# A two-level Winograd kernel: the first partial sum of seven gate stages copied into PSUM by ScalarE, their products reordered and the inner sums spread

## The chip, the cores and the metric

The kernel runs on one core of one Trainium2 chip. A core has TensorE (PE in the profile; its weight loads are PEld), VectorE (DVE), ScalarE (ACT), GpSimd (POOL) and SyncE (SP, which issues most transfers). Each engine runs its own instructions in order and waits for others on semaphores. TensorE writes its products to PSUM, eight banks of 512 fp32 values in each of 128 partitions; VectorE and ScalarE read them there.

The metric is the device time of one execution in microseconds (us), as the median of several runs.

## The reference

All inputs are fp32. For 8 batches of 8 heads, 576 tokens and a head dimension of 64:

```python
kv  = einsum('bhsd,bhse->bhde', k, v)
out = einsum('bhsd,bhde->bhse', q, kv)
x   = out / sqrt(mean(out * out, axis=-1) + 1e-6) * g_norm   # then as (4608, 512)
a, b = x @ w1, x @ w2                                        # (4608, 1024) each
result = (a * b @ w3) @ w_out                                # (4608, 512)
```

## The kernel before, in words

**Stages.** The kernel first multiplies `w3` and `w_out` into one matrix `w3o` of 1024 x 512. The 4608 tokens are then worked in nine groups T of 512 tokens. Groups 0 to 7 hold the first 512 tokens of each batch, group 8 the 64 left over from every batch; the order is 0 to 6, then 8, then 7. For each group there are the two gates (`x @ w1`, `x @ w2`, multiplied elementwise into `ab`) and a projection (`ab` times `w3o`). The attention of batch T + 1 runs in pieces between the products of group T, by the callback `between`.

**One-level gates.** `gates(T, p, ...)` makes two of the eight blocks of 128 gate columns, p and p + 4, with `winograd` (lines 698 to 746): the 2 x 2 blocks c11, c12, c21, c22 from seven products in place of eight. Each product is four matmuls of 128x128 weights by 256 tokens (eight rows in the profile) and fills one bank: one half for `w1`, one for `w2`. A product may be added to what another left in its bank. `keep` (L726) is a copy of a bank to SBUF by ScalarE. `done` calls `multiply`: for a sum of two partial sums VectorE adds them (L859) and multiplies the two halves (L860); where the whole sum is in one bank, ScalarE copies one half (L854) and VectorE multiplies it with the other (L856). The seven products use three banks, r1, r2 and r3, out of a pool of five that hands them out in turn.

**The seven groups with two levels.** In the groups T = 2 to 6, 8 and 7 (`IN_TWO`) p = 2 is made first with one level, then p = 0 and 1 with two levels (`gates_of_two`), and at last p = 3 with one level. Only this last stage is touched. Before the change its order on PE is

```python
a11 b11 -> r1, copied by ScalarE (p1);  s1 t1 -> r2, copied (p5);  s2 t2 added to r1, copied (u2)
# between(): in T = 2 to 5 the next batch's k v products (L335) and their six copies (L343, L345)
s4 b22 added to r2, c12 done;  s3 t3 added to r1, c22 done (adds p5 and r1);  a12 b21 -> r3, c11 done (adds r3 and p1)
a22 t4 added to r1, c21 done
```

**The sums behind.** The projection of these groups (`project_twice`, matmuls at L1223) has two levels too: seven outer products n = 0 to 6, each with seven inner ones of blocks of 128. For that VectorE forms the outer sums of p = 3 (`sum_ab`, L766 and L767), the last of the outer sums of p = 0 to 2 (`of_two`, L1072; the others are L1069 to L1071), and the inner sums of each outer operand (`sum_inner`, L1181 to L1185: three sums s1, s2, s4, and one block replaced by a difference). `sum_inner(0)` belongs to c11, `sum_inner(1, 2)` to the outer sums s1 and s2 in double width. The dictionary `following` (line 1487) says which of them run after which of the four blocks is done.

**What sets the order.** PE, POOL and SP run in the order in which the code is written. In these stages VectorE does too (`manual_schedule`). ScalarE's instructions are placed by the scheduler; the copies that belong to the attention (L294, L296 and L308 for q and x, L343 and L345 for k v) are hung behind certain copies of the gates (`run_slot`).

Of the kernel before, what the change touches and what calls it, by code (L numbers as in the profile page):

```python
# [22 lines left out]
def kernel(  # L23
# [32 lines left out]
    nc = tc.nc  # L56
# [27 lines left out]
    def bank(pool, tag):  # L84
        return pool.tile([P, 512], FP32, name=tag, tag=tag)
# [433 lines left out]
    def run_slot(key, behind):  # L519
        for f, *args in slots.pop(key, []):  # L520
            with tc.issue_after(behind.ins):
                f(*args)
# [174 lines left out]

    def winograd(
        lhsT, rhs, chunks, done, between=lambda: None, keep_u3=True, after=lambda: None,
        places=(2, 1, 0),  # L700
    ):


        def product(a_name, b_name, to=None):
            ps = to if to is not None else bank(ps_mm, "mm").rearrange("p (u n) -> p u n", u=2)
            for u in range(2):
                for c in range(chunks):
                    nc.tensor.matmul(  # L708
                        ps[:, u, :],
                        lhsT=lhsT(a_name, u, c),  # L710
                        rhs=rhs(b_name, c),

                        start=(u == 0 and c == 0 and to is None),
                        stop=(c == chunks - 1),
                        skip_group_check=True,
                    )
            after()
            return ps

        def keep(name, ps):  # L720
            if name == "p1":
                t = pair_of_sums[:, 0].rearrange("p s c t -> p (s c) t")
            else:
                t = late_slots(places[("p5", "u2", "u3").index(name)])
            t = t[:, 0:4, :].rearrange("p (u a) n -> p u (a n)", u=2)
            copies.setdefault(name, []).append(nc.scalar.copy(t, ps))  # L726
            run_slot((stage[0], name), copies[name][-1])
            late[name] = t
            return t

        r1 = product("a11", "b11")
        p1 = keep("p1", r1)
        r2 = product("s1", "t1")
        p5 = keep("p5", r2)
        product("s2", "t2", r1)
        u2 = keep("u2", r1)
        between()
        product("s4", "b22", r2)
        done("c12", r2, u2)
        product("s3", "t3", r1)  # L740
        done("c22", p5, keep("u3", r1) if keep_u3 else r1)
        r3 = product("a12", "b21")
        done("c11", r3, p1)
        between()
        product("a22", "t4", r1)
        done("c21", r1, None)
# [84 lines left out]
    def sum_ab(p):  # L831
        aa[p] = {f"a{i + 1}{j + 1}": ab[j][:, p, i, :] for i in range(2) for j in range(2)}
        return sums(aa[p], free["ab", p])
# [10 lines left out]
    def gates(T, p, between, ready=lambda name: None):  # L844
        def done(name, one, two):
            multiply(name, one, two)
            ready(name)

        def multiply(name, one, two):

            dst = ab[int(name[1]) - 1][:, p, int(name[2]) - 1, :]
            if two is None:
                c = late_pool.tile([P, N], FP32, name="c21")
                copied = nc.scalar.copy(c, one[:, 0, :])  # L854
                run_slot((stage[0], name), copied)
                adds.setdefault(name, []).append(nc.vector.tensor_mul(dst, c, one[:, 1, :]))  # L856
                return
            c = late_pool.tile([P, 2, N], FP32, name="c")
            adds.setdefault(name, []).append(nc.vector.tensor_add(c, one, two))  # L859
            nc.vector.tensor_mul(dst, c[:, 0, :], c[:, 1, :])  # L860

        winograd(
            lambda name, w, c: wa[p][name][:, w, c, :],
            lambda name, c: xb[T][name][:, c, :],
            NP // 2, done, between, T == 0 or p + 1 < NF,
            places=(2, 1, 0) if T not in IN_TWO else (0, 1, 2) if p + 1 == NF else (2, 0, 1),
        )


# [287 lines left out]

    inner = {}

    def sum_inner(*ns, between=lambda: None):  # L1160

        x_1 = ab[1].rearrange("p f j n -> p j f n")
        if ns == (1, 2):
            x = two_ab_sums[0]
        elif ns == (5, 6):
            x = x_1
        else:
            n, = ns
            x = {0: ab[0][:, :, 0], 3: ab_sums[2], 4: ab[0][:, :, 1], 6: x_1[:, 1]}[n].unsqueeze(1)
        a11, a12, a21, a22 = (  # L1170
            x[:, :, 2 * j:2 * j + 2, i * P:(i + 1) * P] for i in range(2) for j in range(2)
        )
        if len(ns) == 2:
            s1, s2, s4 = (pair_of_sums[:, :, i] for i in range(3))
        else:
            s1, s2, s4 = (
                t.unsqueeze(1) for t in (
                    inner_sums[n % 4 // 3] if n < 6 else [pair_of_sums[:, 0, i] for i in range(3)]
                )
            )  # L1180
        nc.vector.tensor_add(s1, a21, a22)  # L1181
        nc.vector.tensor_sub(s2, s1, a11)
        nc.vector.tensor_sub(s4, a12, s2)
        between()
        nc.vector.tensor_sub(a21, a11, a21)  # L1185
        for i, n in enumerate(ns):
            inner[n] = [t[:, i] for t in (a11, a12, a22, s1, s2, s4, a21)]

    def project_twice(T, last, ahead, load_after):
        def store(half):  # L1190
# [245 lines left out]
    for n, T in enumerate(groups):  # L1436
# [44 lines left out]
        for p in range(NF):  # L1481
            if T in IN_TWO and p + 1 < NF:
                continue
            stage[0] = f"p{p}" if T in IN_TWO or T == FIRST_OF_TWO - 1 else None
            if T and p + 1 == NF:
                sum_1, sum_2, sum_4, sum_3 = sum_ab(p)
                following = {
                    "c12": [], "c22": [sum_1], "c11": [lambda: sum_inner(0, between=sum_2)],
                    "c21": [*of_two, lambda: sum_inner(1, 2), sum_3, sum_4],
                }  # L1490
                if T not in TWICE:
                    in_order = tc.manual_schedule(engines={mybir.EngineType.DVE})
                    in_order.__enter__()
                gates(T, p, between, lambda name: all_of(f() for f in following[name]))
                continue
            gates(T, p, between if T or p else lambda: None)
            if T == 0:

                def begin_early(behind):
                    t = early.pop(0)  # L1500
                    with tc.issue_after(behind.ins):
                        next(t)
                    next(t)

                if p == 0:
                    begin_early(copies["xT"])
                if p + 1 < NF:
                    ops = sum_w(p + 1)
                    if p != 2:
                        ops.pop(0)()  # L1510
                    with tc.issue_after(adds["c12"][p].ins):
                        run(ops)
                for n in range(2):
                    if len(converted) < len(todo):
                        ahead = [copies["p5"][p] if p else copies["xT"], copies["u3" if p == 1 else "u2"][p]][n]
                        with tc.issue_after(ahead.ins):
                            begin_next()
                        if len(begun) < len(todo):
                            with tc.issue_after(adds["c12"][0].ins):
                                if p:  # L1520
                                    for c in begun[len(converted)]:
                                        next(c)
                                else:
                                    end_next()
                if p == 0:
                    begin_early(copies["u3"][0])
                if p + 1 == NF:
                    allocate_projection()
                    first, *others = zip(*(f(i) for i in range(NF) for f in (sum_ab, combine_w3o)))
                    with tc.issue_after(adds["c21"][p - 2].ins):  # L1530
                        all_of(step() for step in first)
                    with tc.issue_after(adds["c12"][p - 1].ins):
                        all_of(step() for steps in others for step in steps)
            else:
                ops = [step() for step in sum_ab(p)]
                with tc.issue_after(ops[-1].ins):
                    if p == 1:
                        prepare_some(3)
# [52 lines left out]
```

## Time and profile before

| | |
|---|---|
| runs | 746.61 us median of 3 (745.99 to 747.71) |
| the profiled execution | 747.45 us, of which the span from first to last instruction is 745.7 us |
| granted TensorE clock | 1.000 |
| PE busy | 737.3 us (99%), 6843 matmul rows |
| VectorE busy | 632.7 us (85%), 1212 instructions |
| ScalarE busy | 371.2 us (50%), 638 instructions |
| mean DMA rate | 228 GB/s |

The windows view around the stage that is touched, in T = 3: its first three products, the k v products, its last four products, and the projection. The columns after the window are its length and the busy time of PE, PEld, VectorE, ScalarE and POOL with the number of instructions, then the granted clock, the DMA share and GB/s:

```profile
350.98:356.16 5.18, 5.18 (x26) 4.38 (x24) 5.15 (x12) 3.07 (x6) 0.00 (x0) 1.00 0.92 338
356.16:357.46 1.30, 1.30 (x73) 1.14 (x73) 1.30 (x3) 1.30 (x3) 0.00 (x0) 1.00 0.69 277
357.46:364.47 7.01, 7.01 (x38) 6.19 (x33) 5.92 (x11) 2.81 (x8) 0.00 (x0) 1.00 0.85 153
364.47:386.35 21.88, 21.88 (x197) 21.88 (x196) 20.70 (x42) 8.40 (x12) 0.00 (x0) 1.00 0.91 313
```

PE is busy in all of each window. A busy share is an average, and matmuls are pipelined with modelled ends: a matmul that starts late can still look busy, so the length of a stage of equal matmuls is a second thing to compare. In the views of waits a line reads: who waited, for whom, us in total, times, longest. In the views in order of time it reads: start, duration, engine, source line, operation, what it writes from what, form, and in brackets the idle time before it with what ended it.

### The profile page before, as it was taken

Reading aid. Unit: us, or ns where it says so; the run is one execution under the profiler, and the core shown is the slowest. Engines: PE = TensorE matmul, PEld = TensorE weight load, DVE = VectorE, ACT = ScalarE, POOL = GpSimd, SP = SyncE. Lnnn points to the kernel's source line nnn. Section 1 sums busy time; section 2 is a strip of 40 time slices with the busy share of each in tenths; the row PEclk is TensorE's granted clock in tenths of the full one; section 3 lists DMA queues with packets and bytes.
Section 4 is the critical chain, followed back from the end, with each engine's and each line's share of the span. In section 5 each row is a group of like instructions: output and inputs, shape, how many; then the busy total and the mean of one; then the engine's idle time right before and its main releaser. Section 6 shows DMA issues by size and latency. Waiting matters only on the chain.

```text
span 745.7 us, 16769 instructions
## 1 busy us (share of the span) xinstructions
PE 737.3 (99%) x6843; PEld 658.5 (88%) x6843; DVE 632.7 (85%) x1212; ACT 371.2 (50%) x638; POOL 21.5 (3%) x29
## 2 busy tenths in 40 slices
PE   8999999999999999999999999999999999999998
PEld 5455788888899999999999999999999999999997
DVE  6987998967868699979996999799969987997797
ACT  6687878414552575256526752575267313212321
POOL 0000000131000000010000000000001000000000
PEclk9999999999999999999999999999999999999999
DMA  9996934598999689968987898579847672465454
GB/s 310 365 308 215 263 107 122 124 333 288 275 310 329 172 218 268 312 165 233 276 284 169 252 295 270 179 240 265 290 107 218 209 224 87 157 228 166 133 199 136
DMA packets 135456, 169.65 MB, mean 228 GB/s; under 512 B 78036, under 2 KB 110804, under 8 KB 135380
## 3 DMA queue, kind: packets, MB, share of 16 engines
q1 hardware_dynamic: 132928, 154.16, 68.9%
q10 hardware_dynamic: 2452, 14.42, 5.6%
q8 instruction: 54, 0.88, 0.5%
q14 instruction: 22, 0.18, 0.1%
HBM read 130.55 MB, written 20.71 MB: 203 GB/s over the span
## 4 chain that ended last, share of the span: by engine, by line
PE 94%; DMA 2%; DVE 1%; ACT 1%; issue 0%; SPq 0%; ACTq 0%; DVEq 0%
PE mm L708 38%; PE mm L1223 22%; PE mm L976 21%; PE mm L682 7%; PE at L335 2%; PE at L413 1%; DMA raw<-in_moe_w_out_dram 1%; PE at L669 1%; DMA w3o_sb<-w3o_l 1%; PE mm L413 1%; DMA raw<-in_moe_w_dram 0%; PE at L1266 0%; PE at L432 0%; ACT w_sb L133 0%; DVE c L859 0%; ACT qT L296 0%
## 5 line engine op out<-in xcount | busy, mean ns | idle before, releaser
L1025 ACT COPY slots<-mm 128x512 f32<-128x512 f32 x88 | 51.6, 586 | 131.4 <-PE mm L1223 73.4
L708 PE MATMUL mm<-xT,w_sb 128*128 128x256 f32 x480 | 110.2, 379 | 0.0
L708 PEld LDWEIGHTS mm<-xT,w_sb 128*128 128x128 f32 x480 | 90.4, 190 | 12.1 <-issue 0.5
L708 PE MATMUL mm<-xc,ws 128*128 128x256 f32 x352 | 79.8, 380 | 0.9 <-ACT inner_sums L726 0.9
L708 PEld LDWEIGHTS mm<-xc,ws 128*128 128x128 f32 x352 | 66.9, 190 | 10.2 <-ACT inner_sums L726 1.3
L726 ACT COPY slots<-mm 128x512 f32<-128x512 f32 x61 | 35.8, 587 | 70.9 <-PE mm L708 66.7
L682 PE MATMUL mm<-chunks,ab 128*128 128x512 f32 x128 | 60.7, 605 | 1.2 <-DVE chunks L172 1.2
L1029 DVE TENSOR_TENSOR slots<-mm,slots 128x512 f32<-128x512 f32 x66 | 45.3, 686 | 17.7 <-PE mm L976 17.3
L1026 ACT COPY slots<-mm 128x384 f32<-128x384 f32 x88 | 42.4, 482 | 24.9 <-PE mm L1223 22.3
L976 PE MATMUL mm<-ws,w3o_sb 128*128 128x128 f32 x350 | 54.0, 275 | 0.0
L1223 PE MATMUL mm<-w3o_sb,ab 128*128 128x128 f32 x368 | 48.7, 275 | 0.2 <-DMA w3o_sb<-w3o_l 0.2
L976 PEld LDWEIGHTS mm<-ws,w3o_sb 128*128 128x128 f32 x350 | 46.4, 192 | 0.0
L1223 PEld LDWEIGHTS mm<-w3o_sb,ab 128*128 128x128 f32 x368 | 45.4, 192 | 0.8 <-issue 0.4
L381 DVE TENSOR_REDUCE inv<-sq 128x8 f32<-128x512 f32 (+1 forms) x40 | 24.5, 628 | 25.3 <-ACT sq L380 25.0
L1223 PE MATMUL mm<-w3o_sb,raw 128*128 128x128 f32 x340 | 43.5, 275 | 0.0
L708 PE MATMUL mm<-xc,w_sb 128*128 128x256 f32 x176 | 42.4, 384 | 0.3 <-ACT slots L726 0.3
L682 PEld LDWEIGHTS mm<-chunks,ab 128*128 128x128 f32 x128 | 21.6, 190 | 22.9 <-issue 14.3
L1223 PEld LDWEIGHTS mm<-w3o_sb,raw 128*128 128x128 f32 x340 | 40.7, 192 | 0.0
L708 PE MATMUL mm<-xT,ws 128*128 128x256 f32 x160 | 38.5, 384 | 0.0
L708 PEld LDWEIGHTS mm<-xc,w_sb 128*128 128x128 f32 x176 | 32.8, 190 | 5.3 <-ACT slots L726 0.7
L1030 DVE TENSOR_TENSOR slots<-mm,slots 128x384 f32<-128x384 f32 x66 | 36.4, 551 | 0.9 <-PE mm L1223 0.9
L854 ACT COPY c<-mm 128x256 f32<-128x256 f32 x22 | 8.2, 371 | 54.1 <-PE mm L708 51.2
(230 smaller groups left out, 1634.2 us busy)
## 6 DMA issues: line engine op xcount, KB each, us to landing
w3o_sb<-w_l SPq DMA_DIRECT2D x21, 896.0 KB, 5.3
w3o_sb<-w3o_l SPq DMA_DIRECT2D x18, 896.0 KB, 4.7
raw<-in_moe_w_dram SPq DMA_DIRECT2D x31, 512.0 KB, 7.8
raw<-w3o_l SPq DMA_DIRECT2D x15, 896.0 KB, 4.8
w3o_sb<-w3o_l ACTq DMA_DIRECT2D x14, 896.0 KB, 4.7
k_sb<-in_k_dram SPq DMA_DIRECT2D x16, 576.0 KB, 4.9
v_sb<-in_v_dram SPq DMA_DIRECT2D x16, 576.0 KB, 6.1
q_sb<-in_q_dram SPq DMA_DIRECT2D x32, 256.0 KB, 4.5
```

The lines of the kernel that those rows point to most:

```text
L335: nc.tensor.matmul(ps[r * D:(r + 1) * D, :], lhsT=k_sb[rows, r, cols], rhs=v_sb[rows, r, cols], start=(j == 0), stop=(j == JS - 1),)
L381: adds["norm"] = nc.vector.tensor_reduce(out=inv[:, i], in_=sq.rearrange("p (h d) -> p h d", d=D), axis=AX.X, op=ALU.add)
L413: nc.tensor.matmul(o_ps[l][tokens, n * D:(n + 1) * D], lhsT=qT[r][rows, e, i, tokens], rhs=kv_b[rows, m // 2 ^ l, e, h, :], start=True, st ...
L682: nc.tensor.matmul(sums_ps[half][m], lhsT=w3T[half, c][:, m, :], rhs=chunks[:, c, 1, :], start=(c == 0), stop=(c == KF - 1),)
L708: nc.tensor.matmul(ps[:, u, :], lhsT=lhsT(a_name, u, c), rhs=rhs(b_name, c),  start=(u == 0 and c == 0 and to is None), stop=(c == chunks ...
L726: copies.setdefault(name, []).append(nc.scalar.copy(t, ps))
L976: nc.tensor.matmul(ps[place // 4][:, place % 4, :], lhsT=x, rhs=y, start=new and place // 4 not in seen, stop=True, skip_group_check=True,)
L1025: nc.scalar.copy(z[:, 0:4], ps[0])
L1026: return nc.scalar.copy(z[:, 4:7], ps[1][:, 0:3])
L1029: nc.vector.tensor_add(z[:, 0:4], ps[0], z[:, 0:4])
L1030: nc.vector.tensor_add(z[:, 4:7], ps[1][:, 0:3], z[:, 4:7])
L1223: nc.tensor.matmul(ps[place // 4][:, place % 4, :], lhsT=x[:, c, :], rhs=y[:, c, :], start=new and place // 4 not in seen, stop=(c == 1), ...
```

## The change

In the last one-level gates of the seven groups (`copy_first`), the products run in another order. `a11 b11` goes to r1, ScalarE copies it into r3, another PSUM bank, and `a12 b21` is then added there by PE, so that c11 lies whole in one bank and is made as c21 is: a copy of one half by ScalarE and a multiplication by VectorE. The order of the blocks becomes c11, c22, c12, c21 (before: c12, c22, c11, c21). `sum_inner` is split into steps, and the inner sums of the outer operands 0, 1 and 2 are made one by one (before: 0 alone, 1 and 2 together) and set between the other work after each block, as the new `following` lists. The copy of P1 in SBUF is gone. Line numbers of the changed kernel that matter: L712 matmuls of `winograd`, L739 the copy into r3, L880 and L882 a block from one bank, L885 and L886 a block from two, L1216 to L1219 the steps of an inner sum, L1262 the projection's matmuls.

```diff
--- before.py
+++ after.py
@@ -697,12 +697,16 @@
 
     def winograd(
         lhsT, rhs, chunks, done, between=lambda: None, keep_u3=True, after=lambda: None,
-        places=(2, 1, 0),
+        places=(2, 1, 0), copy_first=False, first=None,
     ):
 
 
-        def product(a_name, b_name, to=None):
-            ps = to if to is not None else bank(ps_mm, "mm").rearrange("p (u n) -> p u n", u=2)
+        def halves(ps):
+            return ps.rearrange("p (u n) -> p u n", u=2)
+
+        def product(a_name, b_name, to=None, new=False):
+            new = new or to is None
+            ps = halves(bank(ps_mm, "mm")) if to is None else to
             for u in range(2):
                 for c in range(chunks):
                     nc.tensor.matmul(
@@ -710,7 +714,7 @@
                         lhsT=lhsT(a_name, u, c),
                         rhs=rhs(b_name, c),
 
-                        start=(u == 0 and c == 0 and to is None),
+                        start=(u == 0 and c == 0 and new),
                         stop=(c == chunks - 1),
                         skip_group_check=True,
                     )
@@ -727,6 +731,28 @@
             run_slot((stage[0], name), copies[name][-1])
             late[name] = t
             return t
+
+        if copy_first:
+            r1 = halves(first if first is not None else bank(ps_mm, "mm"))
+            r3 = halves(bank(ps_mm, "mm"))
+            product("a11", "b11", r1, new=True)
+            copies["p1"].append(nc.scalar.copy(r3, r1))
+            run_slot((stage[0], "p1"), copies["p1"][-1])
+            r2 = product("s1", "t1")
+            p5 = keep("p5", r2)
+            product("s2", "t2", r1)
+            u2 = keep("u2", r1)
+            between()
+            product("a12", "b21", r3)
+            done("c11", r3, None)
+            product("s3", "t3", r1)
+            done("c22", p5, r1)
+            product("s4", "b22", r2)
+            between()
+            done("c12", r2, u2)
+            product("a22", "t4", r1)
+            done("c21", r1, None)
+            return
 
         r1 = product("a11", "b11")
         p1 = keep("p1", r1)
@@ -864,6 +890,8 @@
             lambda name, c: xb[T][name][:, c, :],
             NP // 2, done, between, T == 0 or p + 1 < NF,
             places=(2, 1, 0) if T not in IN_TWO else (0, 1, 2) if p + 1 == NF else (2, 0, 1),
+            copy_first=T in IN_TWO and p + 1 == NF,
+            first=None,
         )
 
 
@@ -1157,7 +1185,7 @@
 
     inner = {}
 
-    def sum_inner(*ns, between=lambda: None):
+    def steps_of_inner(*ns):
 
         x_1 = ab[1].rearrange("p f j n -> p j f n")
         if ns == (1, 2):
@@ -1166,7 +1194,10 @@
             x = x_1
         else:
             n, = ns
-            x = {0: ab[0][:, :, 0], 3: ab_sums[2], 4: ab[0][:, :, 1], 6: x_1[:, 1]}[n].unsqueeze(1)
+            x = {
+                0: ab[0][:, :, 0], 1: ab_sums[0], 2: ab_sums[1], 3: ab_sums[2], 4: ab[0][:, :, 1],
+                6: x_1[:, 1],
+            }[n].unsqueeze(1)
         a11, a12, a21, a22 = (
             x[:, :, 2 * j:2 * j + 2, i * P:(i + 1) * P] for i in range(2) for j in range(2)
         )
@@ -1175,16 +1206,24 @@
         else:
             s1, s2, s4 = (
                 t.unsqueeze(1) for t in (
-                    inner_sums[n % 4 // 3] if n < 6 else [pair_of_sums[:, 0, i] for i in range(3)]
+                    [pair_of_sums[:, n % 2, i] for i in range(3)] if n in (1, 2, 6)
+                    else inner_sums[n % 4 // 3]
                 )
             )
-        nc.vector.tensor_add(s1, a21, a22)
-        nc.vector.tensor_sub(s2, s1, a11)
-        nc.vector.tensor_sub(s4, a12, s2)
-        between()
-        nc.vector.tensor_sub(a21, a11, a21)
         for i, n in enumerate(ns):
             inner[n] = [t[:, i] for t in (a11, a12, a22, s1, s2, s4, a21)]
+        return [
+            lambda: nc.vector.tensor_add(s1, a21, a22),
+            lambda: nc.vector.tensor_sub(s2, s1, a11),
+            lambda: nc.vector.tensor_sub(s4, a12, s2),
+            lambda: nc.vector.tensor_sub(a21, a11, a21),
+        ]
+
+    def sum_inner(*ns, between=lambda: None):
+        *others, replace = steps_of_inner(*ns)
+        all_of(f() for f in others)
+        between()
+        replace()
 
     def project_twice(T, last, ahead, load_after):
         def store(half):
@@ -1484,7 +1523,14 @@
             stage[0] = f"p{p}" if T in IN_TWO or T == FIRST_OF_TWO - 1 else None
             if T and p + 1 == NF:
                 sum_1, sum_2, sum_4, sum_3 = sum_ab(p)
+                zero, one, two = (steps_of_inner(n) for n in range(3)) if T in IN_TWO else [None] * 3
                 following = {
+                    "c11": zero[0:3], "c22": [],
+                    "c12": [sum_1, sum_3, sum_2, one[0], zero[3], one[1]],
+                    "c21": [
+                        one[2], one[3], *of_two, two[0], sum_4, two[1], two[2], two[3],
+                    ],
+                } if T in IN_TWO else {
                     "c12": [], "c22": [sum_1], "c11": [lambda: sum_inner(0, between=sum_2)],
                     "c21": [*of_two, lambda: sum_inner(1, 2), sum_3, sum_4],
                 }
```

## The prediction

> **What bounds the kernel now.** I read the page's busy shares first (PE 99%, DVE 85%), then the windows view of the long steady part, then what PE waited for, then the chain of waits. From 182 to 742 us the windows view gives PE 559.79 us of busy time in 560.00: nothing is left there to win but 0.2 us. The list of PE's waits is short, and only its last line lies in the groups that are changed:
>
> ```profile
> PE mm L682 <- DVE chunks L172: 1.2, 1, 1.2
> PE mm L708 <- ACT inner_sums L726: 0.9, 1, 0.9
> PE mm L708 <- ACT slots L726: 0.3, 1, 0.3
> PE mm L1223 <- DMA w3o_sb<-w3o_l: 0.2, 1, 0.2
> ```
>
> One more loss hides in busy time. In the chain, each projection of 196 matmul rows takes 21.88 us, save one:
>
> ```profile
> 511.41 21.88 PE mm L1223 x196
> ...
> 583.80 22.22 PE mm L1223 x196
> ```
>
> Those 0.34 us, in the group that ends the attention work (T = 6), are matmuls that wait for an inner sum. So the change can gain about 0.34 us, and whatever it makes PE wait for is lost at full price, since everything after is queued on PE.
>
> The stage that is changed is the last one-level gates of seven groups (T = 2, 3, 4, 5, 6, 8, 7). I number its seven products P1 to P7 in PE's order. For T = 3 PE, ScalarE and VectorE stand in order of time like this (start, duration):
>
> ```profile
> 357.46 1.99 PE L708 MATMUL mm<-xT,ws 128*128 128x256 f32 x8
> 359.29 3.62 PE L708 MATMUL mm<-xT,w_sb 128*128 128x256 f32 x16
> 362.75 1.89 PE L708 MATMUL mm<-xc,w_sb 128*128 128x256 f32 x8
> ```
> ```profile
> 355.21 0.58 ACT L726 COPY slots<-mm 128x512 f32<-128x512 f32 x1 [0.77 <-DVE ab L1062]
> ...
> 357.12 2.00 ACT L296 COPY qT<-q_sb 128x1024 uint16<-128x1024 uint16 x2
> ...
> 359.90 0.42 ACT L345 COPY kv_sb<-at 64x64 f32<-64x64 f32 x2
> 364.67 0.37 ACT L854 COPY c<-mm 128x256 f32<-128x256 f32 x1 [4.35 <-PE mm L708]
> ```
> ```profile
> 358.32 0.94 DVE L1071 TENSOR_TENSOR ab<-ab 128x768 f32<-128x768 f32 x1
> 359.56 0.69 DVE L859 TENSOR_TENSOR c<-mm,slots 128x512 f32<-128x512 f32 x1 [0.30 <-PE mm L708]
> ...
> 361.22 0.69 DVE L859 TENSOR_TENSOR c<-slots,mm 128x512 f32<-128x512 f32 x1 [0.51 <-PE mm L708]
> ...
> 366.07 0.41 DVE L856 TENSOR_TENSOR ab<-c,mm 128x256 f32<-128x256 f32 x1
> ```
>
> P4 starts at 357.46, P5 at 359.29, P7 at 362.75. ScalarE is busy with attention copies until 360.32. VectorE has just caught up with PE: it is free at 359.26 and waits 0.30 for P4. P7 writes the bank r1 from which VectorE reads c22 (the row at 361.22, after P5): it ends at 361.91, 0.84 before P7. That margin is what the change spends.
>
> **Part 1, the copy into PSUM and P4.** The copy of P1 stays one ScalarE instruction in the same place; only its target changes. PSUM to PSUM is not in this trace. Nearest rows: 0.585 (L726, same size to SBUF) and, above, 1.05 (L294, twice the elements). ScalarE idles 0.77 before the row at 355.21, so any price up to 1.35 moves nothing behind it, and P4 needs it only at 357.46, four us on. I take 0.585 and a cost of nothing; beyond 1.35 each excess delays all of ScalarE's later copies. The 56 matmul rows of the stage are the same, so PE's own time is the same. Bank order: the projection's second product takes the banks of r3 and r2, free by then; r1's is not needed until the next group.
>
> **Part 2, c11 through ScalarE.** Before, c11 was a 0.72 step of addition (0.69 plus 0.03 to the dependent one) and a multiplication. Now ScalarE copies one half (L854 row: 0.37) and VectorE multiplies (L856 row: 0.41). The build's order puts this copy behind the six kv copies, in the four groups that have them (T = 2 to 5). Those end at 287.38, 360.32, 434.17 and 507.10. VectorE runs in written order and its next instruction is that multiplication: it stands still for about 1.5 us (359.26 to 360.74).
>
> **Part 3, three sums ahead of c22.** After the multiplication come the first three inner sums of c11, then c22's addition. From the rows of such sums in this group (L1181 364.13, L1182 364.59, L1183 365.05, and the next independent one at 365.39) a dependent step costs 0.46 and an independent one 0.34. So multiplication to start of c22's addition: 0.45 + 0.46 + 0.46 + 0.34 = 1.71, and the addition takes 0.69. For T = 3: 360.32 + 0.37 copy + 0.05 hand-over (a norm's square ends on ScalarE at 346.90, VectorE's reduction starts at 346.94) + 1.71 + 0.69 = 363.14. P7 wants the bank at 362.75. The restart has a price too: where PE waited in T = 6, VectorE's sum (start 588.94, 0.68) ended at 589.62, the weight load began at 589.68, and the two waits there cost 0.34 together; the first matmul effectively starts 0.16 after VectorE ends. Stall: 363.14 + 0.16 - 362.75 = 0.55. With the other groups' own rows (end of kv copies + 2.82 + 0.16, less P7's start):
>
> - T = 2: 290.36 - 289.77 = 0.59
> - T = 4: 437.15 - 436.54 = 0.61
> - T = 5: 510.08 - 509.52 = 0.56
>
> Four groups: 2.31 us. In T = 6, 8, 7 there are no kv copies, ScalarE is idle when P4 ends, and the limit is VectorE's backlog: free at 579.81, 647.70 and 715.65 (starts of the L859 rows that follow L1071 without idle time). Adding 1.71 + 0.69 + 0.16 = 2.56: 582.37 against 581.91 (0.46), 650.26 against 650.20 (0.06), 718.21 against 718.14 (0.07). Together 0.59. All stalls: 2.90.
>
> **Part 4, the sums behind.** VectorE loses the 0.72 addition of c11 and the pair of four double sums (0.72, 0.72, 0.60, 0.60), and gets eight single ones at 0.34 to 0.46. That is even, and off PE's path. The dates: in T = 3 the projection's first product starts at 364.47 and needs the replaced block 12 rows of 0.223 later, at 367.15; the new order finishes it near 366.60, and the stall moves PE's date 0.55 further. Its second and third products read sums that end 1 to 2 us ahead. In T = 6 the third sum of the s1 block, late before at 589.02, ends near 586.6: the 0.34 us come back. c21's multiplication comes after six more sums, but nobody waits for its bank.
>
> **Part 5, moved calls.** The second call of between comes after P6 as before; the first after P3 as before. SP's and POOL's orders of instructions are unchanged, so are their transfers.
>
> Sum: +2.31 + 0.59 - 0.34 = **+2.56 us**. The profiled execution had a span of 745.70 and a time of 747.45; it would become 748.26 and 750.0. The median of the runs, 746.61, lies 0.84 under that execution, so I predict 746.61 + 2.56 = 749.2.
>
> The Trainium skill, "Perfetto Trace Analysis", section Optimizing Scalar/DVE Operations, speaks against part 2: it gives VectorE about 60 ns of access overhead on SBUF and 125 ns on PSUM. The rows here disagree: the multiplication with a PSUM input (L856) takes 414 ns, the one from SBUF (L860) 424 ns. By the page the stalls would be some 65 ns longer in each of seven groups, an estimate of 749.6.
>
> **Bounds.** Low: ScalarE rows overlap by 0.1 (364.94 follows a row that ends at 365.04) and the restart is free: 0.26 less in each of four groups, 0.16 less in T = 6, nothing in the last two: 2.90 - 1.04 - 0.16 - 0.13 - 0.34 = +1.2, 747.8. High: c22's addition pays the dependent 0.46, the hand-over 0.11 (as from PE, whose P4 ends at 359.45, to the VectorE row at 359.56) and the restart as much as the visible gap of 0.3 in PE's waits: 0.12 + 0.06 + 0.14 = 0.32 more in seven groups, +4.8, 751.4. The middle values come from rows of the same shapes, so I keep them.
>
> **Rivals.**
> - *The wait at P7 doesn't form* (not slower). Place: c22's addition. It decides if that addition ends by 362.59 in T = 3, 0.55 earlier than I have it; for this ScalarE would have to take c11's copy ahead of its kv copies (then it starts near 359.5, 0.8 sooner). For it: ScalarE's row shows 4 us idle later, so the room is there. Against: the build's order has the copy behind them, and T = 6 stalls without any. Then only the 0.34 returns: 746.3. 15%.
> - *ScalarE is pushed.* If the copy into PSUM takes 2.0 us, it eats the 0.77 of idle time and 0.65 more, and the kv copies and c11's copy move by that in four groups: 2.56 + 2.6 = +5.2, 751.8. For it: no row shows such a write. Against: 0.585 for the same elements, 1.05 for twice as many. 10%.
> - *VectorE relieved, PE faster beyond the measurement.* It would need 1.5 us; PE's visible and hidden losses after 182 us are 0.2 + 0.34. 3%.
>
> **How the numbers follow.** Forecast 72%, 747.8 to 751.4. What a measurement of this kernel can tell from no change is about 0.2%, 1.5 us: 748.1 is the upper bound of the same. The forecast lies above it but for a twelfth (72 - 6 = 66), the second rival wholly (10): slower 76%. Same: 15 + 6 = 21%. Faster 3%. For 8 in 10 I reach from 746.9, into the first rival's upper reaches, to 751.8: left out are some 12 of the first rival's 15, the 3, and 5 above.
>
> **What would show it.** In the changed profile PE's waits gain a line "PE matmul of winograd <- DVE addition of c22" seven times, some 2.9 us in all, four or five of them near 0.5; VectorE waits for ScalarE's c in four groups, about 1.5 us each; the T = 6 projection is back to 21.88; ScalarE's PSUM-to-PSUM row reads near 0.585. Wrong would be: no such line (first rival), or stalls of over 1 us (ScalarE later than I have it).

## The result and the profile after

| | before | after |
|---|---|---|
| median of 6 runs each, side by side | 746.76 us (745.99 to 747.71) | 749.83 us (748.6 to 750.19) |
| ratio | | 1.0038, 95% interval 1.0025 to 1.0051 |
| profiled execution, of which span | 747.45 / 745.7 us | 749.83 / 747.7 us |
| from the first touched stage to the end | 467.66 us | 470.20 us |

The ratio makes the change cost 2.8 us (1.9 to 3.8). The spans of the two profiled executions differ by 2.0 only, because what runs ahead of the change differs by itself: P1 of T = 2 starts at 277.49 us after and at 278.00 before. The last row of the table leaves that out. It is the windows view from P1 of T = 2, the first touched instruction, to the end of the span (columns as before: window, length, busy time of PE, PEld, VectorE, ScalarE and POOL, clock, DMA share, GB/s). Of the kernel after:

```profile
277.49:747.69 470.20, 465.35 (x4418) 439.86 (x4416) 400.48 (x814) 205.87 (x369) 7.83 (x10) 1.00 0.70 213
```

And of the kernel before:

```profile
278.00:745.66 467.66, 464.25 (x4418) 440.70 (x4416) 403.83 (x793) 203.24 (x362) 7.83 (x10) 1.00 0.71 214
```

The same 4418 matmul rows at the same clock take 2.54 us longer, while VectorE is 3.35 us less busy. PE's busy time rises by 1.10, though its work is the same: a part of the loss is again hidden in busy time.

What PE waited for, in the kernel after (who waited, for whom, us, times, longest):

```profile
PE mm L712 <- DVE c L885: 1.5, 5, 0.3
...
PE mm L1262 <- DMA w3o_sb<-w3o_l: 1.0, 1, 1.0
```

The weight loads of the same matmuls, in the same view:

```profile
PEld mm L712 <- DVE c L885: 3.8, 7, 0.8
```

The first line is new. L885 is the addition of two partial sums, c22's here, and L712 is `winograd`'s matmul. The second line is an older loss outside the change, in the projection of T = 1. The chain of waits of the kernel after, at T = 4 and T = 6:

```profile
437.06 0.61 DVE c L885
437.71 1.99 PE mm L712 x8
439.70 21.88 PE mm L1262 x196
...
583.44 0.61 DVE c L885
584.09 1.99 PE mm L712 x8
586.09 21.88 PE mm L1262 x196
```

The end of the kernel now hangs on c22's addition in these groups: it is followed by P7 (8 rows) and the projection. The projection of T = 6 is back at 21.88 us from 22.22.

T = 3 in order of time. PE, of which the rows are P4 with P5, then P6, P7 and the first rows of the projection:

```profile
357.56 3.72 PE L712 MATMUL mm<-xT,w_sb 128*128 128x256 f32 x16
361.11 1.89 PE L712 MATMUL mm<-xT,ws 128*128 128x256 f32 x8
363.30 1.99 PE L712 MATMUL mm<-xc,w_sb 128*128 128x256 f32 x8 [0.29 <-DVE c L885]
365.13 1.50 PE L1262 MATMUL mm<-w3o_sb,ab 128*128 128x128 f32 x12
```

ScalarE in the same stretch: P1's copy into PSUM, then the last kv copy, then c11's half:

```profile
353.00 0.57 ACT L739 COPY mm<-mm 128x512 f32<-128x512 f32 x1 [1.25 <-PE mm L712]
...
359.99 0.42 ACT L345 COPY kv_sb<-at 64x64 f32<-64x64 f32 x2
360.44 0.37 ACT L880 COPY c<-mm 128x256 f32<-128x256 f32 x1
```

VectorE:

```profile
358.41 0.95 DVE L1099 TENSOR_TENSOR ab<-ab 128x768 f32<-128x768 f32 x1
360.84 0.42 DVE L882 TENSOR_TENSOR ab<-c,mm 128x256 f32<-128x256 f32 x1 [1.49 <-ACT c L880]
361.30 0.42 DVE L1216 TENSOR_TENSOR raw<-ab 128x256 f32<-128x256 f32 x1
361.76 0.43 DVE L1217 TENSOR_TENSOR raw<-raw,ab 128x256 f32<-128x256 f32 x1
362.22 0.42 DVE L1218 TENSOR_TENSOR raw<-ab,raw 128x256 f32<-128x256 f32 x1
362.56 0.68 DVE L885 TENSOR_TENSOR c<-slots,mm 128x512 f32<-128x512 f32 x1
```

Read from the bottom: c22's addition ends at 363.24 and P7 starts at 363.30. Ahead of the addition stand three inner sums (L1216 to L1218) and c11's multiplication (L882), and that has waited 1.49 us for a ScalarE copy that started 0.03 after the last kv copy. P6 to P7 takes 363.30 - 361.11 = 2.19 where undisturbed products follow each other at 1.73, and P7 to the projection takes 1.83: 0.46 + 0.10 = 0.56 us lost. The bracket shows only 0.29 of it, since P6's row ends by its model at 363.00 although the next product could have started at 362.84, and the slower first matmul of P7 counts as busy.

Measured so, by the starts of P6, P7 and the projection, P7 is late by 0.61, 0.56, 0.62, 0.56, 0.45, 0.04 and 0.06 us in T = 2, 3, 4, 5, 6, 8 and 7: 2.90 us. Less the 0.34 that T = 6 gains, that is 2.56 of the 2.54 found.

### The profile page after: what moved, and what is told of

Its sections match the earlier page's. It is cut to its first block, busy times and chain, and to the rows that moved or that the text cites. A ratio compares the mean times of both kernels' runs of the same rounds, so it can differ in the third digit from the quotient of the medians.

```text
span 747.7 us, 16794 instructions
## 1 busy us (share of the span) xinstructions
PE 738.9 (99%) x6843; PEld 658.5 (88%) x6843; DVE 629.7 (84%) x1233; ACT 374.0 (50%) x645; POOL 21.9 (3%) x29
## 4 chain that ended last, share of the span: by engine, by line
PE 84%; DVE 6%; ACT 6%; DMA 2%; issue 1%; SPq 0%; ACTq 0%
PE mm L712 32%; PE mm L1262 22%; PE mm L1004 17%; PE mm L682 7%; PE at L335 2%; ACT xT L308 1%; ACT qT L296 1%; PE at L413 1%; DMA raw<-in_moe_w_out_dram 1%; DMA w3o_sb<-w3o_l 1%; DVE xn L390 1%; PE at L669 1%; PE mm L413 1%; ACT slots L730 1%; DMA raw<-in_moe_w_dram 1%
## 5 line engine op out<-in xcount | busy, mean ns | idle before, releaser
L712 PE MATMUL mm<-xT,w_sb 128*128 128x256 f32 x480 | 110.6, 380 | 0.0
L712 PEld LDWEIGHTS mm<-xT,w_sb 128*128 128x128 f32 x480 | 90.0, 190 | 12.3 <-issue 0.5
L712 PE MATMUL mm<-xc,ws 128*128 128x256 f32 x352 | 79.6, 379 | 0.0
L712 PEld LDWEIGHTS mm<-xc,ws 128*128 128x128 f32 x352 | 66.9, 190 | 9.1
L1262 PE MATMUL mm<-w3o_sb,ab 128*128 128x128 f32 x368 | 48.7, 275 | 1.0 <-DMA w3o_sb<-w3o_l 1.0
L1262 PEld LDWEIGHTS mm<-w3o_sb,ab 128*128 128x128 f32 x368 | 45.4, 192 | 1.6 <-DVE raw L1086 1.1
L712 PE MATMUL mm<-xc,w_sb 128*128 128x256 f32 x176 | 43.0, 387 | 1.7 <-DVE c L885 1.5
L1262 PE MATMUL mm<-w3o_sb,raw 128*128 128x128 f32 x340 | 43.5, 275 | 0.0
L1262 PEld LDWEIGHTS mm<-w3o_sb,raw 128*128 128x128 f32 x340 | 40.7, 192 | 0.0
L712 PEld LDWEIGHTS mm<-xc,w_sb 128*128 128x128 f32 x176 | 32.2, 190 | 8.8 <-DVE c L885 3.8
L880 ACT COPY c<-mm 128x256 f32<-128x256 f32 x29 | 10.8, 372 | 54.7 <-PE mm L712 51.7
L712 PE MATMUL mm<-xT,ws 128*128 128x256 f32 x160 | 38.1, 381 | 0.0
```

The lines of the kernel that those rows point to most:

```text
L712: nc.tensor.matmul(ps[:, u, :], lhsT=lhsT(a_name, u, c), rhs=rhs(b_name, c),  start=(u == 0 and c == 0 and new), stop=(c == chunks - 1), s ...
L1262: nc.tensor.matmul(ps[place // 4][:, place % 4, :], lhsT=x[:, c, :], rhs=y[:, c, :], start=new and place // 4 not in seen, stop=(c == 1), ...
```

## The experiments

Each is an edit of the kernel after. "P7 late" and "projections late" are taken from the starts of the matmuls as above; "to the end" is the length from P1 of T = 2 to the end of the span. The ratios are against the kernel before, run beside each (746.76 us for the kernel after, 747.79 for e1 to e4, 747.59 for e5 and e6).

| kernel | ratio (95%) | P7 late, us | projections late, us | to the end, us |
|---|---|---|---|---|
| before | | 0 | 0.34 | 467.66 |
| after | 1.0038 (1.0025 to 1.0051) | 2.90 | 0 | 470.20 |
| e1, sums behind c22 | 0.9993 (0.9984 to 1.0002) | 0 | 0 | 467.32 |
| e2, bank freed by ScalarE | 0.9993 (0.9984 to 1.0002) | 0 | 0 | 467.33 |
| e3, one sum more | 1.0073 (1.0060 to 1.0087) | 6.12 | 0 | 473.70 |
| e4, k v products behind P4 | 1.0002 (0.9992 to 1.0011) | 0.52 | 0 | 467.87 |
| e5, copy alone | 0.9992 (0.9983 to 1.0001) | 0 | 0 | 467.32 |
| e6, sums as before | 1.0020 (1.0011 to 1.0029) | 0 | 1.54 | 468.84 |

**e1: the three inner sums behind c22.** If VectorE's order is what makes c22 late, the sums' place decides.

```diff
-                    "c11": zero[0:3], "c22": [],
+                    "c11": [], "c22": zero[0:3],
```

> The three inner sums of c11 run after c22's addition and multiplication instead of ahead of them; nothing else differs from the changed kernel. Theory (P7 waits for c22's addition, which the sums delay): the addition starts 0.46 + 0.46 + 0.46 us earlier, as soon as P5 is done, the wait at P7 goes from 2.86 us over seven groups to nothing (under 0.1 us), the T = 6 projection stays at 21.88 us, and the time is about 746.4 us (749.8 less 2.9, and 0.34 under the kernel before). Rival 1 (the wait comes from the copy into PSUM or from adding to a bank that ScalarE wrote): P7 is as late as in the changed kernel, 749.8 us. Rival 2 (VectorE is too loaded by the single sums): part of the wait appears later, in the projection, and the time stays above 748.5 us.

It took 747.18 us. VectorE in T = 3 of e1:

```profile
360.87 0.42 DVE L882 TENSOR_TENSOR ab<-c,mm 128x256 f32<-128x256 f32 x1 [1.50 <-ACT c L880]
361.33 0.69 DVE L885 TENSOR_TENSOR c<-slots,mm 128x512 f32<-128x512 f32 x1
```

And its PE:

```profile
362.85 1.89 PE L712 MATMUL mm<-xc,w_sb 128*128 128x256 f32 x8
```

The wait of 1.50 us for ScalarE's copy is still there and costs nothing: the addition ends at 362.02 and P7 starts at 362.85 without a bracket. All 2.90 us are gone, although the copy into PSUM and the product added to it are still there: it was not these that made P7 late.

**e2: the bank freed by ScalarE.** This leaves c22's addition as late as it is and takes away only what P7 shares with it. ScalarE copies r1 to SBUF and the addition reads the copy.

```diff
-            done("c22", p5, r1)
+            done("c22", p5, keep("u3", r1))
```

> ScalarE copies r1 to SBUF after P5 and c22's addition reads the copy; VectorE's order is that of the changed kernel, the sums still ahead of c22. Theory: r1 is then freed by ScalarE, which is idle after c11's copy, so P7 does not wait although c22's addition is as late as before; time about 746.4 to 747.0 us, for 0.59 us of ScalarE seven times off PE's path. Rival 1 (copy into PSUM, bank written by ScalarE): 749.8 us. Rival 2 (VectorE's load as such): 749.8 us, since VectorE does the same work.

It took 747.10 us. In T = 3 of e2, ScalarE:

```profile
361.28 0.59 ACT L730 COPY slots<-mm 128x512 f32<-128x512 f32 x1 [0.49 <-PE mm L712]
```

VectorE:

```profile
362.54 0.68 DVE L885 TENSOR_TENSOR c<-slots 128x512 f32<-128x512 f32 x1
```

PE:

```profile
362.81 1.89 PE L712 MATMUL mm<-xc,w_sb 128*128 128x256 f32 x8
```

The addition starts at 362.54, as late as in the kernel after (362.56), and P7 starts 0.41 us before it ends. A late c22 by itself harms nothing; that it holds r1 does. Seven more ScalarE copies of 0.59 us cost nothing either, since ScalarE idles there.

**e3: one more sum ahead of c22.** The third inner sum is made twice, with the same result, to see whether VectorE's time ahead of the addition passes to the end one for one.

```diff
-                    "c11": zero[0:3], "c22": [],
+                    "c11": [*zero[0:3], zero[2]], "c22": [],
```

> The third inner sum of c11 is made twice, with the same values, ahead of c22: one more step of 0.46 us on VectorE in each of the seven groups. Theory: each P7 is later by 0.46 us, also in T = 8 and 7, where there was next to no slack left: 2.86 + 7 x 0.46 = 6.1 us of waits, time 753.0 us. Rival 1: VectorE has 15% of idle time and takes 3.2 us more of work without an effect, 749.8 us. Rival 2 (a general load on VectorE): a rise, but later than P7, in the projection.

It took 753.29 us, 5.5 us (4.5 to 6.5) over the kernel before. VectorE in T = 3 of e3:

```profile
362.64 0.89 DVE L1218 TENSOR_TENSOR raw<-ab,raw 128x256 f32<-128x256 f32 x2
363.45 0.68 DVE L885 TENSOR_TENSOR c<-slots,mm 128x512 f32<-128x512 f32 x1
```

PE, where this group starts 0.41 later than in the kernel after:

```profile
364.18 1.99 PE L712 MATMUL mm<-xc,w_sb 128*128 128x256 f32 x8 [0.76 <-DVE c L885]
```

P7 is later by 0.45 to 0.47 us in all seven groups than in the kernel after, 3.22 us together, one dependent step of VectorE each. Also in T = 8 and 7, where there were only 0.04 and 0.06 to see, the full 0.51 now shows: the margin there was used up already. To the end it is 473.70, 0.26 us more than 467.66 - 0.34 + 6.12. These lie behind VectorE's last instruction, where the span ends 3.22 us later in e3 and 2.95 in the kernels before and after; why is open.

**e4: the k v products behind P4.** The other half of the wait is ScalarE's queue. If the k v products come after P4, c11's copy can come ahead of the kv copies.

```diff
-            between()
             product("a12", "b21", r3)
             done("c11", r3, None)
+            between()
```

> The first call of between, with the k v products of the next batch in T = 2 to 5, comes after P4 and c11 instead of before P4; ScalarE then copies c11 ahead of its six kv copies. Theory (in four groups ScalarE's queue holds c11 back): c11's copy starts at the end of the q copies, some 1.3 us earlier, c22's addition is limited by P5 alone, and the 2.3 us of T = 2 to 5 go, while the 0.44 + 0.04 + 0.06 of T = 6, 8 and 7 stay: 0.6 us of waits, time 747.4 us. Rival 1: all groups keep their wait, 749.8 us. Rival 2: VectorE is not held up for 1.5 us, but the wait at P7 remains.

It took 747.81 us. ScalarE in T = 3 of e4:

```profile
357.55 2.00 ACT L296 COPY qT<-q_sb 128x1024 uint16<-128x1024 uint16 x2
359.44 0.38 ACT L880 COPY c<-mm 128x256 f32<-128x256 f32 x1
```

VectorE:

```profile
359.86 0.42 DVE L882 TENSOR_TENSOR ab<-c,mm 128x256 f32<-128x256 f32 x1 [0.16 <-ACT c L880]
...
361.67 0.69 DVE L885 TENSOR_TENSOR c<-slots,mm 128x512 f32<-128x512 f32 x1
```

The copy starts 1.0 us sooner than in the kernel after, though this group starts 0.36 later, VectorE stands still for 0.16 in place of 1.49, and the addition ends at 362.36 while P7 starts at 363.19. The four groups with kv copies lose nothing; T = 6, 8 and 7, which have none, keep 0.43, 0.04 and 0.05. This divides the 2.90 us: 2.35 are from the kv copies ahead of c11's copy and 0.55 from VectorE's own backlog. Both need the three sums ahead of c22 as well, as e1 showed. One thing more moves in e4: P4 starts 1.3 us longer ahead of P7, since the k v products now stand behind it. An estimate from the rows says that the kv copies alone are enough: in T = 3 of the kernel after P4 would end at 357.56 + 1.99 = 359.55, so c11's copy could start near 359.65 in place of 360.44, 0.8 us sooner, and no group with kv copies lost more than 0.62. That order was not run.

**e5: the copy into PSUM alone.** The copy of P1 into r3 stays; the products' order and the sums go back to what they were.

```diff
-            product("a12", "b21", r3)
-            done("c11", r3, None)
+            product("s4", "b22", r2)
+            done("c12", r2, u2)
             product("s3", "t3", r1)
             done("c22", p5, r1)
-            product("s4", "b22", r2)
+            product("a12", "b21", r3)
+            done("c11", r3, None)
             between()
-            done("c12", r2, u2)
...
-                    "c11": zero[0:3], "c22": [],
...
-                } if T in IN_TWO else {
                     "c12": [], "c22": [sum_1], "c11": [lambda: sum_inner(0, between=sum_2)],
```

> Only the copy of P1 into PSUM and c11 from one bank are kept; the order of the products and the grouping of the sums are those of the kernel before. Theory: c11's copy comes after P6, when ScalarE has been idle since its kv copies, c22's addition follows P5 without sums ahead of it, so P7 never waits; VectorE loses an addition of 0.72 us ahead of the sums, so the 0.34 us that the T = 6 projection waited in the kernel before are gone: no wait at P7, 21.88 us in that projection, time 0.34 us under the kernel before. Rival (the copy into PSUM or adding to it costs PE something): P7 or P6 late in every group, 2.9 us over the kernel before.

It took 747.12 us. In the chain of waits of e5, the projection of T = 6:

```profile
583.53 21.88 PE mm L1262 x196
```

No product waits, and the 0.34 us of T = 6 are back already: taking c11's addition from VectorE is enough for them.

**e6: the new order of products with the sums as before.** Here the inner sums are grouped as in the kernel before, operand 0 alone behind the third block (c12 here, c11 there) and operands 1 and 2 as a pair behind the fourth, c21.

```diff
-                    "c11": zero[0:3], "c22": [],
-                    "c12": [sum_1, sum_3, sum_2, one[0], zero[3], one[1]],
-                    "c21": [
-                        one[2], one[3], *of_two, two[0], sum_4, two[1], two[2], two[3],
-                    ],
+                    "c11": [], "c22": [],
+                    "c12": [sum_1, lambda: sum_inner(0, between=sum_2)],
+                    "c21": [*of_two, lambda: sum_inner(1, 2), sum_3, sum_4],
```

> The new order of products with the copy into PSUM, but with the sums of the kernel before: those of c11 after c12, the pair of double width after c21. Theory: nothing stands ahead of c22, so P7 does not wait; but c12 is now sixth, its addition starts after P6 (363.0 in T = 3 of the kernel before), and with 0.72, 0.46 and 0.34 us steps behind it the third sum of the pair ends near 369.8 and the replaced block near 370.4, where PE wants them at 369.83 and 370.28: about 0.3 us of waiting inside the second product of each of seven projections, together 2.0 us less the 0.34 of before, 1.7 us over the kernel before. Rival (spreading the sums has no use): no wait in the projections, time 0.34 us under the kernel before. Rival (the order of products itself costs): P7 late as in the changed kernel.

It took 748.83 us, 1.5 us (0.8 to 2.2) over the kernel before. Three projections in its chain of waits:

```profile
584.74 22.10 PE mm L1262 x196
...
652.90 22.10 PE mm L1262 x196
...
721.06 18.98 PE mm L1262 x168
```

Every projection of the seven groups is 0.22 us longer (the last, of 168 rows, has 18.76 elsewhere). VectorE in T = 3 of e6:

```profile
369.33 0.69 DVE L1218 TENSOR_TENSOR inner_sums<-raw,inner_sums 128x512 f32<-128x512 f32 x1
369.94 0.68 DVE L1219 TENSOR_TENSOR raw<-raw 128x512 f32<-128x512 f32 x1
```

PE there:

```profile
369.23 1.56 PE L1262 MATMUL mm<-raw,inner_sums 128*128 128x128 f32 x12
370.68 0.71 PE L1262 MATMUL mm<-raw 128*128 128x128 f32 x4
371.23 1.50 PE L1262 MATMUL mm<-w3o_sb,raw 128*128 128x128 f32 x12
```

The twelve rows read the sums s1, s2 and s4 of a product, four at a time. They take 1.45 us to the next start where others take 1.34, and the four rows after them, on the block that L1219 replaces, 0.55 where others take 0.45. L1218 ends at 370.02, 0.1 before the last four of the twelve would start, and L1219 at 370.62, just ahead of the four at 370.68. So with operand 0 behind c12 the pair in double width comes too late in the new order; spread as in the kernel after or in e1, the sums come in time. Three of them ahead of c22 are not needed, as e1 shows. Whether the pair would be in time with operand 0 behind c22 was not run.

## Why the prediction was right

The forecast was 749.2 us, +2.56; the median is 749.83 and the side-by-side difference 2.8 (1.9 to 3.8). The mechanism is the one that was named: P7 waits for VectorE's addition of c22 to leave r1.

- **Part 1** held. ScalarE's copy from PSUM to PSUM took 570 ns in each of the seven executions of L739, against the 585 assumed, and its row leaves every later copy where it was. The rival in which ScalarE is pushed needed 2.0 us and falls with this row. That a row for PSUM as a target is a little shorter than one for SBUF is also what the Trainium skill says in "ScalarE: Activation LUTs", section Step-by-step: what each stage is for, in its note that ScalarE writes PSUM with lower latency than SBUF; here the difference is 15 ns of 585.
- **Part 2** held. On the clock of the group's own start, 0.10 later than in the kernel before, c11's multiplication was to start at 360.84 and c22's addition to end at 363.24, and they do. VectorE stands still for 1.49 us, as the 1.5 forecast.
- **Part 3** held group by group: 0.59, 0.55, 0.61, 0.56, 0.46, 0.06 and 0.07 forecast, 0.61, 0.56, 0.62, 0.56, 0.45, 0.04 and 0.06 measured. That each was summed from its own group's rows was worth it: the last three have no kv copies and an average over groups would have missed them. e3 confirms the dependent step of 0.46 and e4 the division of 2.31 to 0.59 between the two causes (2.35 to 0.55).
- **Part 4** held: no projection is late, and T = 6 gives back 0.34. e5 shows that this gain needs neither the new order nor the spread sums, which the prediction had put down to the order's dates. Two sizes were a little off: the replaced block of T = 3 ends at 366.79 on the clock of the kernel before, against 366.60 forecast (PE wants it 0.9 us after that), and VectorE's work, called even, fell by 3.35 us.
- **Part 5** held as far as the views show: in the touched groups PE's waits gain no line but c22's.
- **The bounds** were not needed. The restart of 0.16 was right because it had been read from lost time and not from the bracket: P7 starts 0.06 after VectorE's end, and another 0.10 goes into its first matmul. The high bound took 0.30 for it, the visible gap.
- **The rival in which no wait forms** falls by the new line in PE's waits. What it asked for, c11's copy ahead of the kv copies, is e4, and there it does hold for the four groups. **VectorE relieved** falls too: VectorE is 3.35 us less busy and PE gains 0.34.
- **The weighed page.** The Trainium skill's "Perfetto Trace Analysis", Optimizing Scalar/DVE Operations, would have made the stalls some 65 ns longer in each of seven groups for the operand in PSUM. The measured stalls sum to the 2.90 that the rows gave, and L882 from PSUM takes 0.42 us where L886 from SBUF takes 0.43. In e2, c22's addition takes 0.68 us with both operands in SBUF, as in the kernel after with one in PSUM.

One thing in the forecast of the views was wrong: that PE's waits would show the line seven times and some 2.9 us, four or five of them near 0.5. They show 1.5 us in 5, at most 0.3, for the reason read above in T = 3; only the weight loads show all seven, with 3.8 us.

Two readings in the prediction were wrong without touching its sum. Of the listed waits of the kernel before none lies in the changed groups: the 0.2 us for `w3o_sb` are in the projection of T = 1, and from P1 of T = 2 on the list is empty. And the "12 rows of 0.223" of part 4 are 12 matmuls, 24 rows of the profile.

Whether e1, e2 or e5 is faster than the kernel before stays open. To the end of the span each is 0.33 or 0.34 us shorter in one profiled execution, but that is 0.05% of the whole, and each ratio's interval includes 1.

## What to carry to other kernels

When an addition on VectorE is what frees a PSUM bank for the next product, everything moved ahead of it on VectorE's queue, and every copy on another engine that the queue comes to wait for, is paid by TensorE once the margin is gone, as here in all seven groups; so compute the margin group by group before moving anything, and free the bank first. Relieving a busy engine (here 3.35 us of VectorE's time) brought only the 0.34 us of the one result that had been late. A hand-over to another engine can cost by that engine's queue: c11's copy cost time behind the kv copies of four groups, and nothing in e5, where it comes after P6. Where TensorE is near 100% busy, measure a stall by the starts of equal products, since the listed waits showed about half of it here.

## What the runs showed that was not expected

The stretch ahead of the change varied although no edit touches it. In the eight profiled executions the projection of T = 1 lost 0.45, 1.23, 1.09, 2.15, 0.62, 1.68, 1.46 and 1.83 us (before, after, e1 to e6; PE's waits name the transfer that loads `w3o_sb`, and in e2 an addition as well, with 0.2 to 1.6 us in all), and the last stage of T = 1's gates started anywhere from 203.5 to 205.2 us. The two partly make up for each other: P1 of T = 2 starts between 277.44 (e3) and 278.45 us (e4). From the first touched stage on, in contrast, e1, e2 and e5, which differ in code but lose nothing, agree within 0.02 us over 467 us. So in these profiles a change of a few tenths of a us can be read from that stretch, if its end is read apart (the 0.26 us of e3). The medians of whole runs do not resolve it: the intervals of the ratios reach about 0.7 us to either side.
